# The w_out product by Strassen's scheme on half blocks, the last stage's operand split at its store, the forward transform in float32

## The chip, the cores and the metric

The kernel runs on one core of a Trainium2 chip. The metric is the device time of one execution in microseconds; beside it one execution is profiled. A core has a matrix engine (PE, with its weight loads shown apart as PEld), three engines for element-wise work (DVE, ACT, POOL), a queue engine (SP) that issues most transfers, and 16 DMA engines. Matmul results land in PSUM, which has eight banks of 512 float32 columns a partition; all else lies in SBUF. Each engine works through its own list of instructions in order and waits at semaphores.

## The reference

`x` is 8 x 3008 x 256, the two mixing matrices are 256 x 256, `w_in` is 256 x 2048 and `w_out` 2048 x 256, all float32.

```python
X = np.fft.rfft(x, axis=1)
Yr = Xr @ w_r - Xi @ w_i + b_r
Yi = Xr @ w_i + Xi @ w_r + b_i
Yr, Yi = shrink(Yr, 0.01), shrink(Yi, 0.01)     # sign(v) * max(|v| - 0.01, 0)
y = np.fft.irfft(Yr + 1j * Yi, n=3008, axis=1)
h = y.reshape(24064, 256) @ w_in
out = (np.maximum(h, 0.0) ** 2) @ w_out
```

## The kernel before

The transform over 3008 points is done as 64 x 47 points with matrices of cosines and sines. Per batch of 3008 tokens there are four stages. The **forward units** (`Fwd`) add and subtract mirrored inputs on POOL and multiply them with `am`; the result goes to the DRAM tensor `s1`. The **pairs** (`Pair`, twelve per batch) read it back, multiply with `bm`, mix with the weights (`mul`, `mix`), shrink, multiply with `cm` (`back`) and store to `s3`. The **last stage** (`Back`) reads `s3` as `du`, splits it, multiplies with `dx` and leaves `yt`, the transposed input of the feed-forward part. The **feed-forward part** takes tiles of 470 or 376 tokens, seven a batch, and for each tile the 2048 hidden columns in sixteen blocks of 128: `moe_h` multiplies with `win` into a `psh` bank, squares the positive part to `g`, and `moe_o` multiplies `g` with `wout` into two `pso` banks, one per half of the 256 output columns.

Products are made exact enough by splitting: an operand v becomes a rounded `fp32r` part (a cast on ACT) and the rest (a subtraction on DVE or POOL), and a product is three matmuls: high x high, low x high, high x low. So a block costs six matmuls with `win` and six with `wout`, each as wide as the tile.

Batch 0 runs its transform in plain float32 at the start, the front, together with the conversion of the 64-bit weights in 16 parts (`Double`): 12 of the parts are converted there, four beside the first tiles. From then on the tiles of batch b are the main line, and the pairs of batch b+1, the forward units of batch b+2 and the last stage of the next tile are jobs with due times in slots (one slot is one block) that are emitted between the blocks (`pair_tasks`, `fwd_tasks`, `back_tasks`). `moe_o` of a block follows `moe_h` by `LAG` = 2 blocks. A scheduler then sets each engine's order from this emission. The PSUM pools are two `psh` banks, two `pso` banks and four `psf` banks for all transform stages.

Of the kernel before, what the change touches and what calls it, by code (L numbers as in the profile page):

```python
# [29 lines left out]
TILES = (5, 4, 5, 4, 5, 4, 5)  # L30
NF = FF // 128
LAM = 0.01
LAG = 2
NP1 = N1 + 1
AHEAD = 12
FRONT = {"a32": 1, "b32": 1, "w320": 1, "w321": 1, "big": 5, "small": 5, "ka": 5, "xe": 4, "kv": 3}
MAIN = {"xt": 1, "xs": 1, "ksh": 1, "ksl": 1, "duh": 1, "dul": 1, "dy": 1, "xe": 1, "xl": 1, "kv": 1, "xh": 1, "kp": 1, "kq": 1, "mgh": 3, "mgl": 3}
# [3 lines left out]

@with_exitstack
def fnet_moe(ctx: ExitStack, tc, x, w_r, w_i, b_r, b_i, w_in, w_out, am, bm, cm, dm, dx, a32, c32, out):
# [4 lines left out]
    wk = ctx.enter_context(tc.tile_pool(name="wk", bufs=2))  # L48
    cv = ctx.enter_context(tc.tile_pool(name="cv", bufs=1))
    dram = ctx.enter_context(tc.tile_pool(name="dram", bufs=1, space=DRAM))  # L50
    ps_o = ctx.enter_context(tc.tile_pool(name="ps_o", bufs=1, space=PSUM))
    ps_h = ctx.enter_context(tc.tile_pool(name="ps_h", bufs=2, space=PSUM))
    ps_f = ctx.enter_context(tc.tile_pool(name="ps_f", bufs=4, space=PSUM))

    s1 = [dram.tile([G, NP1, 2, D], F32, name=f"s1_{b}") for b in range(B)]
    s3 = [dram.tile([M2, NP, D], F32, name=f"s3_{b}") for b in range(B)]

    am_sb = const.tile([M1, 2, 2, M1], F32R, name="am_sb")
    cm_sb = const.tile([128, G, 256], F32R, name="cm_sb")
    dm_sb = const.tile([M2, 2 * N2], F32, name="dm_sb")  # L60
# [4 lines left out]
    wout = [const.tile([128, NF, D], F32R, name=f"wout{j}") for j in range(2)]  # L65
# [3 lines left out]
    phase = {"pool": front.enter_context(tc.tile_pool(name="front", bufs=2)), "bufs": FRONT}  # L69

    def T(name, shape, dt, tag=None):
        tag = tag or name
        return phase["pool"].tile(shape, dt, name=name, tag=tag, bufs=phase["bufs"].get(tag, 2))

# [39 lines left out]
    def load_consts(g0, g1):  # L114
        pool.dma_start(cm_sb[:, g0:g1], cm[:, g0:g1])


    class Double:
        def __init__(self, hi, lo, src, ins):
            self.hi, self.lo, self.src, self.ins = hi, lo, src, ins  # L120

        def load(self):
            self.st = T("dst", [128, 512, 2], I32, tag="big")
            self.get = nc.sync.dma_start(self.ins(self.st), self.src)
            self.tile = lambda name, dt: T(name, [128, 512], dt, tag="small")

        def load_later(self):
            self.st = cv.tile([128, 512, 2], I32, name="dst", bufs=2)
            load_next(self.ins(self.st), self.src)
            self.tile = lambda name, dt: cv.tile([128, 512], dt, name=name)  # L130

        def bits(self, after):


            self.f = f = self.tile("df", I32)
            self.a = a = self.tile("da", F32)
# [11 lines left out]
        def join(self):  # L148
            self.w = w = self.tile("dw", F32)
# [6 lines left out]
        def split(self):  # L156
            w, hi = self.w, self.hi
            v = w.rearrange("p (f d) -> p f d", f=hi.shape[1]) if len(hi.shape) == 3 else w
            copy(act, hi, v)
            sub(dve, self.lo, v, hi)  # L160

    def moe_part(q):
        if q < 8:
            f, c = divmod(q, 2)
            fs = slice(f * 512, f * 512 + 512)
            return Double(
                win[0][:, c, fs], win[1][:, c, fs],
                w_in[c * 128:(c + 1) * 128, f * 1024:(f + 1) * 1024],
# [522 lines left out]
```

## Time and profile before

| | us |
|---|---|
| median of 3 runs | 2730.65 (2728.38 to 2730.72) |
| the profiled execution | 2727.27 |
| its span in the trace | 2725.5 |
| DVE busy | 1764.8 (65% of the span) |
| ACT busy | 1524.1 (56%) |
| POOL busy | 1058.6 (39%) |

A busy time is the sum of an engine's instructions; the span runs from the first to the last instruction of the program, and the execution takes 1.8 us more than it. A row of a group names the line, engine and operation, the tiles (output <- inputs), the shapes, the count, the busy time with the mean of one in ns, and then the idle time just before them with what ended it. A row of a timeline begins with the start and the length in us. A row of a stretch gives, for PE, PEld, DVE, ACT and POOL, busy us and instructions, then PE's granted clock, the share of the DMA engines and GB/s.

### The profile page before, as it was taken

The numbers are of one execution on the slowest core, as the hardware profiler recorded it, in microseconds if no ns is written. First come the engines' busy times: TensorE is split into PE (matmuls) and PEld (weight loads), VectorE is DVE, ScalarE is ACT, GpSimd is POOL, SyncE is SP. The second block draws the span as 40 slices with busy tenths as digits, with TensorE's granted clock in tenths as the row PEclk, the third lists the DMA queues.
The fourth block names the chain that finished last, engine by engine and source line by source line (L and its number), as shares of the span: only waits on it lengthen the run. The fifth ranks groups of instructions, "written<-read, shape, count | busy, mean of one in ns | idle before, by whom it ended". The sixth has DMA issues, their size and how long they took to land.

```text
span 2725.5 us, 41465 instructions
## 1 busy us (share of the span) xinstructions
PE 2682.9 (98%) x14902; PEld 2479.4 (91%) x14902; DVE 1764.8 (65%) x3050; ACT 1524.1 (56%) x3286; POOL 1058.6 (39%) x1071
## 2 busy tenths in 40 slices
PE   6899999999999999999999999999999999999999
PEld 5688999999999999899998999989999999999998
DVE  5956776667666676666666666666666666655554
ACT  3455565555565555555565555555555555555554
POOL 2144544444443443543534444344444343332200
PEclk8899999999999999999999999999999999999999
DMA  8443321222121221222211122122112111010000
GB/s 267 138 138 90 98 68 55 73 59 73 49 79 52 64 83 41 69 66 68 64 59 56 59 74 65 57 62 76 59 53 62 34 60 47 30 33 28 24 14 13
DMA packets 120356, 181.13 MB, mean 66 GB/s; under 512 B 12679, under 2 KB 90871, under 8 KB 119767
## 3 DMA queue, kind: packets, MB, share of 16 engines
q1 hardware_dynamic: 119271, 174.53, 21.1%
q0 software_dynamic: 880, 3.96, 0.5%
q8 instruction: 117, 1.92, 0.3%
q14 instruction: 88, 0.72, 0.1%
HBM read 103.07 MB, written 75.37 MB: 65 GB/s over the span
## 4 chain that ended last, share of the span: by engine, by line
PE 92%; DVE 3%; DMA 2%; issue 1%; POOL 1%; ACT 1%; SPq 0%; ACTq 0%; POOLq 0%; DVEq 0%
PE psh L458 38%; PE pso L480 38%; PE psf L263 7%; PE psf L240 3%; PE psf L297 2%; PE psf L215 2%; PE psf L439 1%; PE psf L434 1%; PE psf L438 1%; DMA xt<-x_in 1%; POOL xs L190 0%; DMA x<-x_in 0%; DVE df L143 0%; DVE dw L150 0%; DMA du<-s 0%
## 5 line engine op out<-in xcount | busy, mean ns | idle before, releaser
L458 PE MATMUL psh<-yt,win 128*128 128x470 f32 (+1 forms) x5376 | 1227.0, 362 | 1.7 <-DVE mg L466 1.1
L458 PEld LDWEIGHTS psh<-yt,win 128*128 128x128 f32 x5376 | 946.6, 189 | 70.3 <-DVE mg L466 3.4
L480 PE MATMUL pso<-mgh,wout 128*128 128x470 f32 (+1 forms) x3584 | 932.4, 359 | 0.0
L81 DVE TENSOR_TENSOR mgl<-mg,mgh 128x470 fp32r<-128x470 f32 (+1 forms) x896 | 650.3, 726 | 394.8 <-ACT mgh L77 367.5
L466 DVE SCALAR_TENSOR_TENSOR mg<-psh,mr 128x470 f32<-128x470 f32 (+1 forms) x896 | 539.8, 603 | 433.9 <-ACT mr L465 427.5
L77 ACT CAST mgh<-mg 128x470 fp32r<-128x470 f32 (+1 forms) x896 | 495.7, 553 | 473.8 <-DVE mg L466 469.8
L465 ACT ACTIVATE mr<-psh 128x470 f32<-128x470 f32 (+1 forms) x896 | 474.4, 530 | 419.4 <-PE psh L458 411.1
L480 PEld LDWEIGHTS pso<-mgh,wout 128*128 128x128 f32 x3584 | 653.8, 188 | 51.1 <-ACT mgh L77 0.2
L480 PE MATMUL pso<-mgl,wout 128*128 128x470 f32 (+1 forms) x1792 | 581.0, 359 | 1.0 <-DVE mgl L81 1.0
L480 PEld LDWEIGHTS pso<-mgl,wout 128*128 128x128 f32 x1792 | 328.5, 188 | 26.4 <-DVE mgl L81 1.7
L81 POOL TENSOR_TENSOR duh<-du,duh 32x512 fp32r<-32x512 f32 (+1 forms) x141 | 168.9, 1198 | 431.8 <-issue 255.1
L276 POOL TENSOR_TENSOR ke<-ke,bias 128x512 f32<-128x512 f32 x84 | 109.1, 1298 | 365.3 <-ACT ke L77 364.7
L81 POOL TENSOR_TENSOR dul<-du,duh 64x256 fp32r<-64x256 f32 x251 | 221.6, 883 | 31.6 <-PE psf L439 14.6
L263 PE MATMUL psf<-wx,kxh 128*128 128x256 f32 x1008 | 226.5, 282 | 0.0
L81 POOL TENSOR_TENSOR yt<-dy,yt 128x376 fp32r<-128x376 f32 (+1 forms) x141 | 134.9, 956 | 234.7 <-ACT yt L77 218.2
L190 POOL TENSOR_TENSOR xs<-xt 120x512 f32<-120x512 f32 (+1 forms) x98 | 131.4, 1340 | 176.9 <-DVE xl L81 74.2
L263 PEld LDWEIGHTS psf<-wx,kxh 128*128 128x128 f32 x1008 | 173.7, 188 | 6.8 <-ACT kxh L77 0.3
L253 POOL TENSOR_TENSOR kp<-kxh 128x256 f32<-128x256 f32 x84 | 65.9, 784 | 287.2 <-ACT kxh L77 259.2
L285 DVE TENSOR_TENSOR kv<-psf,ke 64x256 f32<-64x256 f32 x336 | 141.7, 422 | 30.5 <-PE psf L263 23.3
L263 PE MATMUL psf<-wx,kxl 128*128 128x256 f32 x504 | 141.6, 281 | 0.0
L443 DVE TENSOR_TENSOR dy<-psf,dy 128x188 f32<-128x188 f32 (+1 forms) x282 | 86.5, 325 | 27.6 <-ACT dy L77 22.5
L240 PE MATMUL psf<-kb,ka 128*128 128x128 f32 x672 | 104.0, 275 | 0.0
(85 smaller groups left out, 2398.9 us busy)
## 6 DMA issues: line engine op xcount, KB each, us to landing
s<-ku SPq DMA_DIRECT2D x192, 128.0 KB, 1.8
s<-xe SPq DMA_DIRECT2D x48, 480.0 KB, 3.3
du<-s SPq DMA_DIRECT2D x112, 192.0 KB, 3.0
ka<-s SPq DMA_DIRECT2D x84, 256.0 KB, 2.8
xt<-x_in SPq DMA_DIRECT2D x42, 480.0 KB, 5.3
out<-mo SPq DMA_DIRECT2D x64, 235.0 KB, 2.0
kb<-bm_in SPq DMA_DIRECT2D x84, 128.0 KB, 2.7
out<-mo SPq DMA_DIRECT2D x48, 188.0 KB, 2.0
```

The source lines that it names most:

```text
L77: return act.copy(out=out, in_=in_)
L81: return eng.tensor_tensor(out=out, in0=a, in1=b, op=ALU.subtract)
L190: return eng.tensor_tensor(out=out[:, :n], in0=self.xt[:, :n, 0], in1=self.xt[:, :n, 1], op=(ALU.add, ALU.subtract)[t])
L240: nc.tensor.matmul(pv[:, :, c, g, :], self.a[:, g, c * 128:(c + 1) * 128], bg, start=True, stop=True)
L263: self.last = nc.tensor.matmul(ps, l, wx[j][:, k, c, :], start=n == 0, stop=n == 5)
L276: pool.tensor_tensor(out=self.e, in0=self.e, in1=bias, op=ALU.add)
L285: dve.tensor_add(out=v[64 * r:64 * r + 64, g], in0=ps[gs], in1=self.e[gs, r])
L443: dve.tensor_add(out=y[:, c, :n * W], in0=ps[:, 0, :n * W], in1=y[:, c, :n * W])
L458: nc.tensor.matmul(ps[:, :k], win[w][:, c, fs], y[:, c, :k], start=n == 0, stop=n == 5)
L465: act.activation(r, ps[:, :k], AF.Relu)
L466: dve.scalar_tensor_tensor(out=g, in0=ps[:, :k], scalar=0.0, in1=r, op0=ALU.max, op1=ALU.mult)
L480: nc.tensor.matmul(acc[t][d][:, :k], wout[w][:, f, dsl], g, start=f == 0 and j == 0, stop=f == NF - 1 and j == 2,)
```

## The change

**The w_out product.** The sixteen blocks are taken as eight steps of two (`Step`), the tile's tokens as two halves of h = 252 or 250 (six tiles a batch, `HALF`), and the output as two halves of 128 columns. The 2 x 2 blocks of g (two hidden blocks by two token halves, side by side in `mc`) and of `wout` are multiplied by a scheme of seven products in place of eight: four with sums of g (`ms`: T1, T3, T2, T4, made by three POOL subtractions and additions; split into `mt`), three with plain parts (`mb`). The sums of `wout` (S1 to S4) are made once, in the front (`wout_sums`). The products are summed over the steps in four `pso` banks, and at a tile's end `drain` copies them out and forms the four output blocks by six POOL additions. So the psf banks go from four to two.

```diff
-    def moe_h(t, f):
...
-    def moe_o(t, f):
...
+    class Step:
+        def block(self, j):
...
+            if j == 0:
+                r = T("mr", [128, 2 * HM], F32)[:, :w]
+                act.activation(r, ps, AF.Relu)
+                dve.scalar_tensor_tensor(out=c, in0=ps, scalar=0.0, in1=r, op0=ALU.max, op1=ALU.mult)
+                return
+            act.activation(c, ps, AF.Relu)
+            act.activation(c, c, AF.Square)
...
+            halves(self.raw[0][:, B11], self.raw[1][:, B11], c[:, 0], dve)
+            halves(self.raw[0][:, B21:], self.raw[1][:, B21:], c[:, 2:4], dve)
+            self.s = s = T("ms", [128, 4 * HM], F32)[:, :4 * h].rearrange("p (j h) -> p j h", j=4)
+            pool.tensor_tensor(out=s[:, T1:T3 + 1], in0=c[:, 1::2], in1=c[:, 0:2], op=ALU.subtract)
+            pool.tensor_tensor(out=s[:, T2], in0=c[:, 0], in1=s[:, T3], op=ALU.add)
+            sub(pool, s[:, T4], c[:, 2], s[:, T2])
+        def split(self):
+            halves(self.sum[0], self.sum[1], self.s, dve)
+        def out(self, j):
...
+            products = (
+                ((A12, self.raw, B21, o[0], 0), (S4, self.raw, B22, o[0], 1), (A11, self.raw, B11, o[1], 0)),
+                ((S2, self.sum, T2, o[1], 1), (S1, self.sum, T1, o[2], 0), (S3, self.sum, T3, o[2], 1),
+                 (A22, self.sum, T4, o[3], 0)),
+            )[j]
+            for a, g, b, ps, i in products:
+                for k, (w, v) in enumerate(((0, 0), (1, 0), (0, 1))):
...
+                        mm = nc.tensor.matmul(
                            ps[:, i], wout[w][:, n, a], g[v][:, b], start=first and i == 0,
                            stop=n == NF // 2 - 1 and k == 2 and (i == 1 or a == A22),
                        )
+        def drain(self, j):
...
+            copy(act, e[:, 4:6], o[1])
+            copy(act, e[:, 6:8], o[2])
+            copy(dve, e[:, 2], o[3][:, 0])
...
+            add(u2, u2, p1)
+            add(c22, p5, p7)
+            add(e[:, 6:8], e[:, 6:8], u2.unsqueeze(1).broadcast_to([128, 2, h]))
+            add(e[:, 0:2], e[:, 0:2], e[:, 4::2])
+            add(c22, c22, u2)
+            add(e[:, 2], e[:, 2], p7)
```

`halves(hi, lo, v, eng)` is the cast on ACT and the subtraction on `eng`. The tile `ms` has one buffer, `mc`, `mb` and `mt` have two. `copy(dve, e[:, 0:2], o[0])` empties the first bank half a step earlier.

**The other edits.** `store_back` stores the result of `back` to `s3` already split (ACT cast, DVE subtraction from PSUM, two stores), so `Back.split` with its POOL subtractions goes and `Back.load` reads three pieces; the last stage always works on 188 columns and copies a piece that belongs to the next tile later (`put(1)`). `Fwd.run` multiplies in plain float32 (`am32`) without a split. In `Pair`, the bias is added by DVE from PSUM, the sum for the third product is formed from PSUM (ACT copy, DVE addition) in place of three POOL additions, the split after the shrink goes to POOL, and `cm` is loaded per pair by a transfer that POOL issues (`load_back`) and no longer kept. All 16 weight parts are converted in the front; the four sums of each pair of `wout` parts are four DVE operations of 128 x 256, followed by splits of 256, 512 and 1024 columns a partition. The due times and buffer counts are set anew:

```diff
-                first, step = 1.0, 7.5
+                first, step = 1.0, 6.1
-                    first, step = 31.0, 5.2
+                    first, step = 20.5, 4.6
-    jobs += fwd_tasks(b + 2, 0, 10.0 if b else 30.0, 6.8 if b else 5.0)
+    jobs += fwd_tasks(b + 2, 75.0, 1.4)
-                    jobs += back_tasks(t, tt * NF + 2.5)
+                    jobs += back_tasks(t, NF * j + 0.5)
-        k = n * 9 // 5
+        k = n * 13 // 10
```

**Where instructions now stand.** On PE, in the last batch of the kernel before, the products of a block (`pso`, with the casts `mgh` and the rests `mgl`) and the win product of a later block (`psh`) take turns, six and six:

```order
L480 MATMUL pso_29552<-mgh,wout_100 128x470
L480 MATMUL pso_29552<-mgh,wout_101 128x470
L480 MATMUL pso_29553<-mgh,wout_100 128x470
L480 MATMUL pso_29553<-mgh,wout_101 128x470
L480 MATMUL pso_29552<-mgl,wout_100 128x470
L480 MATMUL pso_29553<-mgl,wout_100 128x470
L458 MATMUL psh<-yt_29219,win_98 128x470
L458 MATMUL psh<-yt_29219,win_99 128x470
L458 MATMUL psh<-yt_29220,win_98 128x470
L458 MATMUL psh<-yt_29219,win_98 128x470
L458 MATMUL psh<-yt_29219,win_99 128x470
L458 MATMUL psh<-yt_29220,win_98 128x470
```

On PE in the last batch of the changed kernel, the products of one step's sums (`mt_32361` is the cast, `mt_32362` the rest) are parted by a whole win product:

```order
L515 MATMUL pso_32155<-mt_32361,wout_84 128x250
L515 MATMUL pso_32156<-mt_32361,wout_83 128x250
L515 MATMUL pso_32156<-mt_32361,wout_84 128x250
L473 MATMUL psh<-yt_32016,win_81 128x500
L473 MATMUL psh<-yt_32016,win_82 128x500
L473 MATMUL psh<-yt_32017,win_81 128x500
L473 MATMUL psh<-yt_32016,win_81 128x500
L473 MATMUL psh<-yt_32016,win_82 128x500
L473 MATMUL psh<-yt_32017,win_81 128x500
L515 MATMUL pso_32154<-mt_32362,wout_83 128x250
L515 MATMUL pso_32155<-mt_32362,wout_83 128x250
L515 MATMUL pso_32155<-mt_32361,wout_83 128x250
```

Counted over the whole order of before, the products of a block start after the win products of two later blocks in 855 of 896 cases, as the text of the program has it. In the changed kernel the plain parts `mb` of a step come two steps' win products after that step's start, but the sums' casts `mt` mostly 3.5 and their rests 4.0, where the text has 3.0.

On ACT before, in the last batch, the relu (`mr`) and the cast (`mgh`) alternate:

```order
L77 CAST mgh<-mg 128x376
L465 ACTIVATE mr<-psh 128x376
L77 CAST mgh<-mg 128x376
L465 ACTIVATE mr<-psh 128x376
L77 CAST mgh<-mg 128x376
L465 ACTIVATE mr<-psh 128x376
```

On ACT in the changed kernel, in the last batch, a step is six instructions, and the cast of the sums (`mt_32251`, of the step two before the one whose plain part is `mb_32359`) stands between the relus of the two blocks:

```order
L480 ACTIVATE mr<-psh 128x500
L89 CAST mb_32304<-mc 128x500
L89 CAST mt_32251<-ms 128x1000
L483 ACTIVATE mc<-psh 128x500
L89 CAST mb_32359<-mc 128x250
L484 ACTIVATE mc<-mc 128x500
L480 ACTIVATE mr<-psh 128x500
L89 CAST mb_32359<-mc 128x500
```

On POOL before, in a batch with pairs and forward units, all is work of the transform: `duh`, `dul` and `yt` of the last stage, `kp`, `kq`, `kxl` and `ke` of a pair, `xs` of a forward unit:

```order
L190 TENSOR_TENSOR xs<-xt 120x512
L81 TENSOR_TENSOR duh<-du,duh 32x256
L81 TENSOR_TENSOR dul<-du,duh 64x256
L81 TENSOR_TENSOR yt_21153<-dy,yt_21152 128x2x188
L276 TENSOR_TENSOR ke<-ke,bias 128x512
L81 TENSOR_TENSOR duh<-du,duh 32x512
```

On POOL in the changed kernel, at a tile's end in a batch with pairs, the three operations on `ms` of every step stand among the additions of `drain` (`me`), a load it issues (`kcm`) and the last stage's `yt`:

```order
L100 DMA kcm<-cm_in 128x512
L493 TENSOR_TENSOR ms<-mc 128x500
L494 TENSOR_TENSOR ms<-mc,ms 128x250
L93 TENSOR_TENSOR ms<-mc,ms 128x250
L539 TENSOR_TENSOR me<-me 128x250 x2
L539 TENSOR_TENSOR me<-me 128x500
L539 TENSOR_TENSOR me<-me 128x250
L493 TENSOR_TENSOR ms<-mc 128x500
L539 TENSOR_TENSOR me<-me 128x500
L539 TENSOR_TENSOR me<-me 128x250
L494 TENSOR_TENSOR ms<-mc,ms 128x250
L93 TENSOR_TENSOR ms<-mc,ms 128x250
```

The additions part the first operation on `ms` from the other two, which come before the cast on ACT.

More of the change, by code (lines that the diff above doesn't have):

```diff
@@ L561, in fnet_moe @@
     with tc.issue_after(ring[-1].folds[1].ins):
-        pool.dma_start(am_sb, am)
         pool.dma_start(dx_sb, dx)
-    chain.append(units[-1].get)
-    load_next(dm_sb, dm)
-    for p in parts[AHEAD:AHEAD + 2]:
-        p.load_later()
+    chain[nc.sync], chain[pool] = units[-1].get, ring[-1].folds[1]
+    front.close()
+    phase.update(
+        pool=ctx.enter_context(tc.tile_pool(name="main", bufs=2)), bufs={**MAIN, "psf": 2, "psh": 2},
+        psum=ctx.enter_context(tc.tile_pool(name="main_ps", bufs=1, space=PSUM)),
+    )
```

455 lines of the change are left out of this document (233 added, 222 removed).

## Prediction

> **What bounds the kernel now.** I read the page's busy line first, then the sums over a stretch in the middle, then the chain that ended last, then the groups.
>
> ```profile
> PE 2682.9 (98%) x14902; PEld 2479.4 (91%) x14902; DVE 1764.8 (65%) x3050; ACT 1524.1 (56%) x3286; POOL 1058.6 (39%) x1071
> 1000.00:1400.00 400.00, 400.00 (x2268) 372.33 (x2267) 263.04 (x449) 231.93 (x496) 172.15 (x173) 1.00 0.21 63
> PE 92%; DVE 3%; DMA 2%; issue 1%; POOL 1%; ACT 1%; SPq 0%; ACTq 0%; POOLq 0%; DVEq 0%
> L458 PE MATMUL psh<-yt,win 128*128 128x470 f32 (+1 forms) x5376 | 1227.0, 362 | 1.7 <-DVE mg L466 1.1
> L480 PE MATMUL pso<-mgh,wout 128*128 128x470 f32 (+1 forms) x3584 | 932.4, 359 | 0.0
> ```
>
> In the stretch from 1000 to 1400 us PE is busy for all 400 us at full granted clock (1.00), with DVE at 66%, ACT at 58%, POOL at 43% and the DMA engines at 21%. The chain is 92% PE. So the middle costs what its matmuls cost, and the first question is their pace. Ends of matmuls are modelled, so I take runs of one kind and divide the time by their number.
>
> ```profile
> 2530.54 2.60 PE psh L458 x12
> 2533.14 2.56 PE pso L480 x12
> 2494.93 2.07 PE psh L458 x12
> 330.38 1.42 PE psf L263 x12
> 64.67 0.61 PE L347 MATMUL psf<-kbb,ka 128*128 128x128 f32 x4
> 65.11 0.60 PE L372 MATMUL psf<-kv,kk 128*128 128x256 f32 x2
> 65.55 1.89 PE L361 MATMUL psf<-w,kx 128*128 128x256 f32 x8
> 67.27 0.61 PE L347 MATMUL psf<-kbb,ka 128*128 128x128 f32 x4
> 1531.01 0.28 PE L438 MATMUL psf<-dx_sb,duh 128*128 128x188 f32 x1
> 1531.12 0.27 PE L439 MATMUL psf<-dx_sb,dul 128*128 128x188 f32 x1
> ```
>
> 470 columns take 215 ns, 376 take 172, 256 take 118: 0.457 to 0.462 ns a column, though every matmul loads new weights. 188 columns take 110 ns (1531.01 to 1531.12), more than their share, so a floor lies just there. Plain float32 is two instructions per product, 215 ns each at 256 columns (eight from 65.55 to 67.27) and 110 at 128 (four from 64.67 to 65.11).
>
> **The change, part by part.** *PE.* win keeps its columns (24064 x 96). wout has as many before, 2.310 million, 1057 us at 0.4575. After it has 48 tiles x 8 steps x 21 matmuls of 252 or 250 columns, 2.021 million, at the 256-wide row's 0.462 ns 934 us: **-123 us**. The width is not in the trace; bounds are 110 ns (the 188 row) and 118 ns, 887 to 951 us. The forward product goes from six matmuls of 256 columns a unit to four float32 instructions: 91 x (4 x 215 - 6 x 118) ns = **+14 us**. The last stage keeps its matmuls nearly (784 to 768). PE's work behind the front is then win 1057, wout 934, pairs 84 x 3.7 = 312 (24 matmuls of 256 columns at 118, eight instructions at 110), forward 78, last stage 768 x 0.11 = 85: 2466 us.
>
> *Front.*
>
> ```profile
> 60.00:90.00 30.00, 28.89 (x152) 25.46 (x151) 29.89 (x75) 15.93 (x45) 0.00 (x0) 1.00 0.76 233
> 117.22 4.90 PE L458 MATMUL psh<-yt,win 128*128 128x470 f32 x12 [0.41 <-ACT yt L77]
> L143 DVE SCALAR_TENSOR_TENSOR df<-da,df 128x512 int32<-128x512 int32 x16 | 11.5, 717 | 0.1
> L142 DVE TENSOR_SCALAR da<-da 128x512 f32<-128x512 f32 x16 | 7.2, 452 | 2.2 <-ACT da L139 2.1
> L81 DVE TENSOR_TENSOR wout<-dw,wout 128x512 fp32r<-128x512 f32 x8 | 6.5, 818 | 0.3 <-ACT wout L77 0.3
> L81 DVE TENSOR_TENSOR kv<-kv,kc 128x256 f32<-128x256 f32 x24 | 10.0, 416 | 0.1
> ```
>
> DVE is full there (29.89 of 30), and the first win product starts at 117 us. All 16 weight parts now stand ahead of it, where 12 did: four more at six operations of 0.45 to 0.72 us, 3.6 together, make 14. Each pair of wout parts gets four 128x256 sums (0.42) and splits of 256, 512 and 1024 columns (0.42, 0.69, about 1.2), 4.0 us; four pairs are 16, for the six wout splits of 0.82 that go. With the two more win splits, DVE gains 27. Before 60 us it idles, which takes some: **+22 us**, between 10 and 30. The same work leaves the main part, where PE covered it: no gain there.
>
> *End.*
>
> ```profile
> 2717.77 3.65 PE pso L480 x17
> out<-mo SPq DMA_DIRECT2D x64, 235.0 KB, 2.0
> ```
>
> PE ends at 2721.4, 4 us before the span. Now the last step's sums and six POOL additions (5.5 us, priced below) stand between with nothing beside them: **+8 us**, 5 to 12. So far -123 + 14 + 22 + 8 = -79: 2646 of span, 2648 with the 1.8 us around it, **if PE stays as full as now**.
>
> *What must stay hidden.* A step (two blocks) needs, per the rows below, 2.8 us of POOL, 1.05 of ACT and 1.2 of DVE in one ring. The tile ms has one buffer: POOL's first subtraction of the next step waits until DVE has read the last sums, DVE waits for ACT's cast, ACT for POOL.
>
> ```profile
> L276 POOL TENSOR_TENSOR ke<-ke,bias x84: 1278/1292/1517, 236.2 to 2375.3; 128x512 f32<-128x512 f32 x84
> L253 POOL TENSOR_TENSOR kp<-kxh x84: 725/741/1192, 226.4 to 2360.8; 128x256 f32<-128x256 f32 x84
> L77 ACT CAST mgh<-mg 128x470 fp32r<-128x470 f32 x512 | 300.9, 588 | 292.5 <-DVE mg L466 290.5 <-PE pso L480 1.1
> L77 ACT CAST mgh<-mg 128x376 fp32r<-128x376 f32 x384 | 194.8, 507 | 181.3 <-DVE mg L466 179.3 <-PE pso L480 0.9
> L81 DVE TENSOR_TENSOR ksl<-kv,ksh x84: 675/692/1781, 243.1 to 2385.5; 128x512 fp32r<-128x512 f32 x84
> L81 DVE TENSOR_TENSOR mgl<-mg,mgh x896: 528/649/1740, 130.2 to 2719.8; 128x470 fp32r<-128x470 f32 x102, 128x376 fp32r<-128x376 f32 x78
> ```
>
> (The first two and the last two are views of one tile: minimum, median and maximum in ns.) POOL: 1.28 for 504 columns and twice 0.74 for 252. ACT: 0.86 ns a column between the two casts, so 1.05 at 1008 (two casts of 504, 1.24, would bound it). DVE: 0.69 at 512 and 0.42 at 256, so 1.21 at 1008 (at most 1.38 as two). Sum 5.0, with five hand-overs of about 0.05 5.3. But DVE and POOL do not run side by side:
>
> ```profile
> 1525.44 0.73 POOL L253 TENSOR_TENSOR kp<-kxh 128x256 f32<-128x256 f32 x1
> 1526.14 1.18 POOL L253 TENSOR_TENSOR kq<-kxl 128x256 f32<-128x256 f32 x1
> 1527.40 0.93 POOL L254 TENSOR_TENSOR kp<-kp,kq 128x256 f32<-128x256 f32 x1
> 1525.68 1.05 DVE L81 TENSOR_TENSOR xl<-xs,xh 120x512 fp32r<-120x512 f32 x1
> 1526.65 1.08 DVE L81 TENSOR_TENSOR mgl<-mg,mgh 128x376 fp32r<-128x376 f32 x1
> ```
>
> Five operations worth 0.74 + 0.69 + 0.74 + 0.53 + 0.74 = 3.44 us alone (mgl at 376 columns by its minimum) fill 1525.44 to 1528.33, 2.89 us: they take turns, and each change of turn gives back 0.14. DVE operations on PSUM do not stretch. The changed step adds 2.31 us of such DVE work (252, 504 and 1008 columns) to POOL's 2.8. DVE's two shorter subtractions fall into POOL's part of the ring: up to 0.82 us more, 5.3 to 6.1; I take the middle, **5.7 us a step**. The Trainium skill, "SBUF — State Buffer", section "Who interferes with whom", says that a DVE instruction with two SBUF inputs and a GpSimd one take a shared port by an exclusive lock for the whole instruction. The turns agree with that, the 0.14 us does not; held whole, it gives the fourth case below.
>
> At a tile's end POOL adds 4 x 0.74 + 2 x 1.28 = 5.5 us. While ACT and DVE work on ms (1.05 + 1.21), POOL has what DVE's turn leaves, some 1.2 us a step, so about 3 us of it lengthen the ring, 0.4 a step. Against this PE: 12 x 504 x 0.4575 + 21 x 252 x 0.462 = 5.21 us a step.
>
> Of 384 steps, by the tables of tasks, the pairs' tasks stand beside 246 (27 of batch 0, 36.5 of each of the next six), the forward units' beside 63 (nine, seven times), neither beside 75.
>
> - *No side work*: PE 5.43 with the last stage, ring 6.1: 0.67 x 75 = **+50 us**.
> - *Pairs*: 5.21 + 3.7/3.05 + 0.22 = 6.65. The ring 6.1, and POOL's further 1.2 us a step (kxl, ksl, yt, issuing a load) fit its free time or collide: 6.1 to 6.6. I take **0**, but this is thin.
> - *Forward units*: PE 6.67; POOL gets 13 x 2 x 0.74 = 19 us in nine steps, 2.1 a step, 0.9 over its room: ring 7.0. The order leaves the sums' products up to a step of slack, so **+10 us** of 22.
>
> Queued behind a waiting POOL subtraction are ksl, kxl, yt and the folds, and PE waits for each.
>
> ```profile
> L77 ACT COPY ke<-psf 128x512 f32<-128x512 f32 x84 | 49.2, 586 | 8.7 <-PE psf L263 7.5
> L115 POOL DMA_DIRECT2D cm_sb<-cm_in x3 | 1.7, 577 | 0.0
> ```
>
> Two psf banks in place of four cost nothing if jobs stay 0.9 slot (2.9 us) apart, since emptying a bank takes 0.6 to 1.4; if each pair stalls once, 84 x 0.6 = 50 us. The 84 loads issued by POOL (0.58 each) are in the 1.2 above. The doubled stores to s3 go to DMA engines that are 21% busy: nothing.
>
> Sum: 2648 + 50 + 10 = **2708 us**, beside 2727.3 of the profiled execution; the median of three, 2730.65, lies 3.4 above that.
>
> **The rivals.** *Everything is absorbed:* the ring runs at 5.3 and PE paces all stages, 2648. For it: no stretch of before shows PE waiting. Against it: the order puts the sums' products later than the program's text does, up to four steps' win products behind, where before they stood at their place.
>
> *The ring paces the pairs too* (slower): DVE carries 2.31 + 0.69 us a step and for each pair eleven operations of 0.42 to 0.69 us, 5.5 together, so 4.8 a step there, and each of its turns waits for POOL's; a late DVE subtraction delays POOL, which delays ACT. It decides from a ring of 6.75: (2733 - 2708) / 246 = 0.10 above 6.65. At 6.95 it costs 74 us, and some 8 more in the forward units: 2790. For it: turns stretch ksl from 0.69 to 1.78 us and mgl to 1.74 at worst, with POOL at 43%.
>
> ```profile
> L81 POOL TENSOR_TENSOR yt<-dy,yt 128x376 fp32r<-128x376 f32 (+1 forms) x141 | 134.9, 956 | 234.7 <-ACT yt L77 218.2
> L287 DVE TENSOR_SCALAR kc<-kv 128x512 f32<-128x512 f32 x84 | 41.5, 494 | 0.1
> ```
>
> *The turns are held whole* (the page's rule as a mechanism of this kernel): per step 2.31 + 2.76 + 0.69 of tile sums + 0.32 of yt (128 x 0.956 / 384) = 6.08, x 384 = 2335; pairs 84 x 3.2 = 270 (kxl 0.74, ksl 1.29, kv 0.69, kc 0.49); folds 135. 2740 behind a front of 139 and an end of 9: 2888. With 0.14 back at six turns a step it is under PE's 2466. The rows speak against it.
>
> *Two banks are too few:* 2708 + 50 = 2758.
>
> *The shorter products gain nothing*, because each weight load (188 ns in the groups) would pace them: the 256-wide row at 118 excludes it.
>
> **How the numbers follow.** Forecast 45% (its own range 2660 to 2730), absorbed 12%, ring in the pairs 28%, two banks 8%, turns held whole 6%, no gain 1%. Range: from the absorbed case, 2650, to a ring of some 7.1, 2830. A measurement of this kernel tells about 0.2% from no change (2725 to 2736). Faster: the absorbed case and nine tenths of the forecast, 0.52. The same: the edges, 0.09. Slower: 0.39.
>
> **What would show it.** wout groups at 8064 matmuls paced near 115 ns; the first win product near 139 us; windows in the pairs with PE over 97% busy and in the last batch near 89%, with PE's weight loads waiting for DVE mt; POOL near 75% busy with its 256-wide operations well above 0.74. It would be wrong if PE's share in the pairs fell below 94% (ring) or if PE waited there for ACT or DVE to empty psf (banks).

## The result, and the profile after

| | before | after |
|---|---|---|
| median | 2729.52 us (2728.08 to 2730.72) | 2941.26 us (2939.76 to 2944.61) |
| ratio | | 1.078 (95%: 1.076 to 1.080) |
| span of the profiled execution | 2725.5 | 2940.7 |

The kernel became 212 us slower. The forecast was 2708, the range ended at 2830. One execution is left out of all that follows, the second of experiment e5: it took 5440 us, twice as long as the first. The first fence is from the page of the changed kernel: the busy line, the engines of the chain that ended last, and three groups.

```profile
PE 2685.1 (91%) x16856; PEld 2406.9 (82%) x16856; DVE 2081.2 (71%) x3035; ACT 1789.2 (61%) x3562; POOL 2012.1 (68%) x2082
...
POOL 34%; PE 30%; DVE 15%; issue 8%; ACT 7%; DMA 1%; SPq 0%; POOLq 0%; DVEq 0%; ACTq 0%
...
L493 POOL TENSOR_TENSOR ms<-mc 128x500 f32<-128x500 f32 (+1 forms) x384 | 502.0, 1307 | 559.8 <-DVE mt L93 557.1
...
L481 DVE SCALAR_TENSOR_TENSOR mc<-psh,mr 128x500 f32<-128x500 f32 (+1 forms) x384 | 260.5, 678 | 387.5 <-POOL ms L93 368.6
...
L539 POOL TENSOR_TENSOR me<-me 128x250 f32<-128x250 f32 (+3 forms) x288 | 288.1, 1018 | 30.0 <-ACT me L89 23.3
```

The chain was 92% PE. Now POOL has 34% of it, and PE 30%, although POOL is busy for only 68% of the span: POOL stands idle for 557 us before L493, until DVE has read the last sums, and DVE for 369 us before L481, until POOL has read the buffer of `mc` that is to be overwritten. Engines that wait for each other hold the kernel with none of them full. The sums over stretches and the list of waits say what that does to PE:

```profile
1000.00:1400.00 400.00, 376.62 (x2432) 342.22 (x2432) 292.08 (x435) 252.37 (x504) 285.54 (x300) 0.97 0.30 89
160.00:2930.00 2770.00, 2584.35 (x16453) 2327.78 (x16452) 1971.28 (x2803) 1727.61 (x3404) 1952.64 (x2028) 0.97 0.27 79
```

```profile
POOL ms L493 <- DVE mt L93: 557.1, 255, 4.8
ACT mt L89 <- POOL ms L93: 474.0, 292, 5.9
DVE mc L481 <- POOL ms L93: 368.6, 258, 6.8
...
PE psh L473 <- DVE mc L481: 91.8, 81, 4.0
```

(A wait is given by total us, number of times and the longest.) The stretch from 1000 to 1400 us had PE busy for 400.00 of 400 at a clock of 1.00; now it is 376.62 at 0.97. From 160 to 2930 us PE is idle for 2770 - 2584 = 186 us. The last row, about half of that, is the end of the chain: `psh` has two banks, the win product needs one emptied by DVE (L481), DVE waits for POOL. The prediction's own sign of being wrong is there too. It named a share of PE under 94% beside the pairs: from 1000 us on it is 94.2%, and in the three stretches of 400 us behind that 92.4 to 92.7%.

**Where in the tile.** From the starts of POOL's first subtraction (L493) in the trace I took the time of every step, and the mean by its place in the tile (batches are counted from 0). The first two places are those beside which POOL forms the output of the tile before.

| mean step, us, by place | 1 | 2 | 3 | 4 | 5 | 6 | 7 | 8 | batch mean |
|---|---|---|---|---|---|---|---|---|---|
| after, batch 4 (pairs beside it) | 8.60 | 10.59 | 6.80 | 6.72 | 6.42 | 7.67 | 6.24 | 6.52 | 7.45 |
| after, batch 7 (nothing beside it) | 7.46 | 7.18 | 5.56 | 5.58 | 5.42 | 5.84 | 6.64 | 5.58 | 6.17 |

Beside the pairs, steps 3 to 8 take 6.7 on average, PE's own pace by the prediction (6.65). The loss stands in the first two. This is POOL's timeline over such a tile end (start, length, and in brackets the idle time before):

```profile
1279.03 1.40 POOL L493 TENSOR_TENSOR ms<-mc 128x504 f32<-128x504 f32 x1 [2.39 <-DVE mt L93]
1280.51 1.06 POOL L494 TENSOR_TENSOR ms<-mc,ms 128x252 f32<-128x252 f32 x1
1281.54 0.99 POOL L93 TENSOR_TENSOR yt<-dy,yt 128x376 fp32r<-128x376 f32 x1
1282.50 0.72 POOL L93 TENSOR_TENSOR ms<-mc,ms 128x252 f32<-128x252 f32 x1
1283.36 0.74 POOL L539 TENSOR_TENSOR me<-me 128x252 f32<-128x252 f32 x1
1285.32 0.80 POOL L539 TENSOR_TENSOR me<-me 128x252 f32<-128x252 f32 x1 [1.22 <-ACT me L89]
1286.08 1.27 POOL L493 TENSOR_TENSOR ms<-mc 128x504 f32<-128x504 f32 x1
1287.32 2.14 POOL L539 TENSOR_TENSOR me<-me 128x504 f32<-128x504 f32 x2
1289.41 0.91 POOL L494 TENSOR_TENSOR ms<-mc,ms 128x252 f32<-128x252 f32 x1
1290.29 1.18 POOL L93 TENSOR_TENSOR kxl<-kp,kxh 128x256 fp32r<-128x256 f32 x1
1291.42 2.37 POOL L539 TENSOR_TENSOR me<-me 128x504 f32<-128x504 f32 x2
1293.75 0.72 POOL L93 TENSOR_TENSOR ms<-mc,ms 128x252 f32<-128x252 f32 x1
1294.42 1.28 POOL L93 TENSOR_TENSOR ksl<-kv,ksh 128x512 fp32r<-128x512 f32 x1
1295.66 1.18 POOL L93 TENSOR_TENSOR yt<-dy,yt 128x8 fp32r<-128x8 f32 x1
1296.86 1.38 POOL L493 TENSOR_TENSOR ms<-mc 128x504 f32<-128x504 f32 x1
```

A step's three operations on `ms` are L493, L494 and L93. At 1279 they end 4.2 us after their start. At 1286 four tile-end additions (L539) and a pair's `kxl` stand in between, and they end 8.4 us after it; the steps that begin at 1279.03 and 1286.08 take 7.05 and 10.78 us. Only after the third may ACT cast, DVE subtract and L481 overwrite `mc`. These are the rows of PE, then of DVE, at that place:

```profile
1281.01 1.54 PE L473 MATMUL psh<-yt,win 128*128 128x504 f32 x6
...
1291.13 0.65 PE L515 MATMUL pso<-mb,wout 128*128 128x252 f32 x4
1293.32 0.77 PE L332 MATMUL psf<-ksh,kcm 128*128 128x256 f32 x4 [1.53 <-DVE dy L445]
1295.24 2.89 PE L473 MATMUL psh<-yt,win 128*128 128x504 f32 x6 [1.16 <-DVE mc L481]
...
1294.50 0.68 DVE L481 SCALAR_TENSOR_TENSOR mc<-psh,mr 128x504 f32<-128x504 f32 x1 [0.98 <-POOL ms L93]
```

POOL's third operation ends at 1294.47, DVE's L481 starts at 1294.50, and PE's win product follows. Its six matmuls take 2.89 us where six took 1.54 at 1281: the clock has fallen. (The first wait, 1.53 us before L332, is put down to DVE's `dy`, which empties a `psf` bank; it is not the ring's own.) The same place in stretches of 2 us, and in two rows cut where the clock changes (the third number from the end is the granted clock):

```profile
1290.00:1292.00 2.00, 1.78 (x16) 1.58 (x14) 2.00 (x2) 0.00 (x0) 2.00 (x3) 1.00 0.04 14
1292.00:1294.00 2.00, 0.68 (x4) 0.56 (x4) 0.62 (x3) 1.25 (x4) 2.00 (x3) 1.00 0.01 2
1294.00:1296.00 2.00, 0.84 (x3) 0.67 (x3) 1.12 (x2) 1.50 (x3) 2.00 (x3) 0.55 0.68 256
1296.00:1298.00 2.00, 2.00 (x7) 1.55 (x6) 1.11 (x2) 0.84 (x3) 1.99 (x2) 0.50 0.00 0
1298.00:1300.00 2.00, 2.00 (x10) 1.97 (x9) 0.68 (x1) 1.43 (x4) 0.24 (x1) 0.50 0.00 0
1300.00:1302.00 2.00, 2.00 (x10) 1.64 (x9) 0.76 (x2) 0.31 (x2) 1.76 (x3) 0.75 0.43 91
1302.00:1304.00 2.00, 2.00 (x20) 2.00 (x19) 1.29 (x2) 1.68 (x3) 0.29 (x1) 1.00 0.94 287
...
1290.80:1294.21 3.41, 1.75 (x13) 1.34 (x11) 1.82 (x4) 1.25 (x4) 3.41 (x4) 1.00 0.06 22
1294.21:1295.24 1.03, 0.00 (x0) 0.00 (x1) 0.68 (x1) 0.74 (x1) 1.03 (x2) 0.50 0.99 376
```

So a wait can cost twice: the idle time, and PE at half speed behind it, here for nearly 7 us. Not every wait does. In the trace's clock records the clock fell to 0.50 at 31 places between 165 and 2905 us, at 23 of them for 3.4 us, 137 us in all, while PE waited over 170 times.

### The profile page after: what moved, and what is told of

It is laid out like the page before. It is cut to its first block, busy times and chain, and to the rows that moved or that the text cites. A ratio compares the mean times of both kernels' runs of the same rounds, so it can differ in the third digit from the quotient of the medians.

```text
span 2940.7 us, 47049 instructions
## 1 busy us (share of the span) xinstructions
PE 2685.1 (91%) x16856; PEld 2406.9 (82%) x16856; DVE 2081.2 (71%) x3035; ACT 1789.2 (61%) x3562; POOL 2012.1 (68%) x2082
## 4 chain that ended last, share of the span: by engine, by line
POOL 34%; PE 30%; DVE 15%; issue 8%; ACT 7%; DMA 1%; SPq 0%; POOLq 0%; DVEq 0%; ACTq 0%
PE psh L473 14%; PE pso L515 10%; POOL ms L493 9%; POOL me L539 7%; DVE mt L93 6%; POOL ms L494 6%; POOL ms L93 6%; ACT mt L89 4%; PE psf L300 3%; POOL xs L232 3%; DVE kv L321 2%; DVE mb L93 2%; POOL ksl L93 2%; DVE mc L481 1%; POOL yt L93 1%
## 5 line engine op out<-in xcount | busy, mean ns | idle before, releaser
L473 PE MATMUL psh<-yt,win 128*128 128x500 f32 (+1 forms) x4608 | 1239.9, 404 | 93.6 <-DVE mc L481 91.8
L493 POOL TENSOR_TENSOR ms<-mc 128x500 f32<-128x500 f32 (+1 forms) x384 | 502.0, 1307 | 559.8 <-DVE mt L93 557.1
L93 DVE TENSOR_TENSOR mb<-mc,mb 128x500 fp32r<-128x500 f32 (+3 forms) x768 | 697.7, 918 | 136.2 <-ACT mb L89 132.9
L515 PEld LDWEIGHTS pso<-mt,wout 128*128 128x128 f32 x4608 | 653.6, 193 | 64.4 <-ACT mt L89 10.5
L515 PE MATMUL pso<-mt,wout 128*128 128x250 f32 (+1 forms) x4608 | 686.2, 285 | 9.9 <-ACT mt L89 8.4
L89 ACT CAST mt<-ms 128x1000 fp32r<-128x1000 f32 (+1 forms) x384 | 395.9, 1031 | 475.2 <-POOL ms L93 474.0
L93 DVE TENSOR_TENSOR mt<-ms,mt 128x1000 fp32r<-128x1000 f32 (+1 forms) x384 | 494.8, 1289 | 109.7 <-ACT mt L89 106.8
L515 PE MATMUL pso<-mb,wout 128*128 128x250 f32 (+1 forms) x3456 | 537.4, 284 | 21.2 <-DVE mb L93 21.1
L481 DVE SCALAR_TENSOR_TENSOR mc<-psh,mr 128x500 f32<-128x500 f32 (+1 forms) x384 | 260.5, 678 | 387.5 <-POOL ms L93 368.6
L515 PEld LDWEIGHTS pso<-mb,wout 128*128 128x128 f32 x3456 | 466.2, 189 | 35.1 <-DVE mb L93 26.1
L93 POOL TENSOR_TENSOR ms<-mc,ms 128x250 f32<-128x250 f32 (+1 forms) x384 | 314.4, 819 | 21.3
L494 POOL TENSOR_TENSOR ms<-mc,ms 128x250 f32<-128x250 f32 (+1 forms) x384 | 307.8, 802 | 22.0
L539 POOL TENSOR_TENSOR me<-me 128x250 f32<-128x250 f32 (+3 forms) x288 | 288.1, 1018 | 30.0 <-ACT me L89 23.3
L93 POOL TENSOR_TENSOR yt<-dy,yt 128x376 fp32r<-128x376 f32 (+3 forms) x168 | 153.1, 917 | 51.2 <-ACT yt L89 46.6
```

What stands on the lines that cost most here:

```text
L89: return act.copy(out=out, in_=in_)
L93: return eng.tensor_tensor(out=out, in0=a, in1=b, op=ALU.subtract)
L473: nc.tensor.matmul(ps, win[k][:, c, fs], y[:, c, :w], start=n == 0, stop=n == 5)
L481: dve.scalar_tensor_tensor(out=c, in0=ps, scalar=0.0, in1=r, op0=ALU.max, op1=ALU.mult)
L493: pool.tensor_tensor(out=s[:, T1:T3 + 1], in0=c[:, 1::2], in1=c[:, 0:2], op=ALU.subtract)
L494: pool.tensor_tensor(out=s[:, T2], in0=c[:, 0], in1=s[:, T3], op=ALU.add)
```

## The experiments

Three theories stood at the start. **Ring**: POOL's additions and sums, DVE's and ACT's splits and the one buffer of `ms` pace the steps. **Port**: POOL and DVE are slowed by each other's turns, whatever the buffers. **Banks**: two `psf` banks make the transform products wait. Ratios are to the kernel before.

| run | us (median) | ratio (95%) |
|---|---|---|
| e1, `ms` with two buffers | 2816.61 | 1.0323 (1.0293 to 1.0353) |
| e2, no tile-end additions | 2714.93 | 0.9945 (0.9923 to 0.9968) |
| e3, eight products, two `psf` banks | 2827.54 | 1.0363 (1.0333 to 1.0393) |
| e4, sums on DVE | 2780.24 | 1.0190 (1.0160 to 1.0219) |
| e5, three tile-end additions on DVE | 2747.07 (one execution) | |
| e6, e1 and e5 together | 2751.37 | 1.0074 (1.0045 to 1.0103) |
| e7, sums on DVE, a split on POOL | 2845.24 | 1.0418 (1.0388 to 1.0448) |
| e8, eight products, four `psf` banks | 2732.76 | 1.0010 (0.9999 to 1.0021) |
| e10, e5 again | 2750.35 | 1.0080 (1.0064 to 1.0097) |
| e11, four tile-end additions on DVE | 2767.31 | 1.0141 (1.0126 to 1.0156) |
| e12, eight products, three `psf` banks | 2732.97 | 1.0016 (1.0007 to 1.0026) |
| e13, after, another order | 2945.22 | 1.0790 (1.0774 to 1.0806) |
| e14, after, a third order | 2943.89 | 1.0784 (1.0768 to 1.0800) |
| e15, e11 in another order | 2773.26 | 1.0159 (1.0144 to 1.0174) |
| e16, e10 in another order | 2805.76 | 1.0279 (1.0262 to 1.0296) |
| e17, e2 in another order | 2709.32 | 0.9925 (0.9910 to 0.9940) |
| e18, e3 in another order | 2826.27 | 1.0352 (1.0337 to 1.0367) |
| e19, e8 in another order | 2732.69 | 1.0011 (1.0002 to 1.0021) |

**e1: `ms` with two buffers** (`ka` and `kcm` give up one each for the room).

```diff
-    ... "mr": 1, "ms": 1, "me": 1,
+    ... "mr": 1, "ms": 2, "me": 1, "ka": 1, "kcm": 1,
```

> Changed kernel with two buffers for ms (room made by one buffer in place of two for ka and kcm, whose loads stay 2.4 and 1.8 slots behind the last read). No work is removed. Ring theory (POOL's three operations on ms, ACT's cast, DVE's subtraction and the wait for the one buffer set the step, and POOL's tile-end additions lengthen it): a step of the last batch falls from 5.72 us to PE's 5.4, the two steps at a tile's end (8.5 and 10 us now, others 6.6) lose part of their excess; 2740 to 2850 us. Port theory (POOL and DVE operations taking turns fill the time, whatever the buffers): the sum of turns is the same, 2900 to 2960.

2817, 125 under after: the ring, and not the turns by themselves, since no operation was taken away and both engines were busy for longer than in after (POOL 2080 us for 2012, DVE 2115 for 2081). 87 of the 212 us stay. My reading, not tried by itself: a second buffer lets one step's sums begin before the last are read, but the additions still stand in POOL's list.

**e2: the six additions at a tile's end left out.**

```diff
-            add(u2, u2, p1)
-            add(c22, p5, p7)
-            add(e[:, 6:8], e[:, 6:8], u2.unsqueeze(1).broadcast_to([128, 2, h]))
-            add(e[:, 0:2], e[:, 0:2], e[:, 4::2])
-            add(c22, c22, u2)
-            add(e[:, 2], e[:, 2], p7)
```

> Changed kernel without the six POOL additions of a tile's end: the output is made of single products. Ring theory: the two long steps at a tile's end (8.5 and 10 us) become ordinary (6.6), 48 x about 5 us = 200 to 250 less, 2690 to 2750 us. Prediction's own step (POOL's additions absorbed beside pairs): only the 75 steps without side work gain, 75 x 0.4 = 30 us, about 2910. Bank theory (PE waits for two psf banks): nothing changes, 2930 to 2945.

2715: **226 us less**, 4.7 us for each of the 48 tiles, with `ms` at one buffer and `psf` at two banks as they were. This run alone would fit the port theory too, since 5.5 us of POOL's work a tile are gone with their turns; e1 and the rows above speak for the ring. The busy line and the main stretch of this run:

```profile
PE 2602.3 (96%) x16856; PEld 2358.9 (87%) x16856; DVE 1996.1 (74%) x3035; ACT 1798.6 (66%) x3562; POOL 1730.4 (64%) x1794
```

```profile
160.00:2700.00 2540.00, 2496.82 (x16434) 2276.03 (x16432) 1883.56 (x2800) 1735.18 (x3402) 1671.59 (x1742) 1.00 0.29 86
```

The matmuls that kept PE busy for 2584 us behind the front take 2497 here, at a clock of 1.00, and PE idles for 2540 - 2497 = 43 us in place of 186. So the 226 us are, within a few us, 143 of waiting and 87 of PE being busy for longer over the same matmuls. The clock accounts for some 65 of these 87: the clock records of these stretches have 142 us at half speed in after and 11 here, and half of the difference is lost. The other 22 are not shown; the ends of matmuls are modelled, so short waits may hide in busy time. The mean step at places 1 and 2 of batch 4 is 6.91 and 6.60 (8.60 and 10.59 in after), the batch mean 6.67 (7.45), and that of batch 7 5.73 (6.17).

**e3, e8, e12: eight products, with two, four and three `psf` banks.** The scheme is undone, all else stays: each step multiplies the four plain blocks with `wout` (twelve matmuls of 504 or 500 columns) into two `pso` banks.

```diff
-            products = (
-                ((A12, self.raw, B21, o[0], 0), (S4, self.raw, B22, o[0], 1), (A11, self.raw, B11, o[1], 0)),
-                ((S2, self.sum, T2, o[1], 1), (S1, self.sum, T1, o[2], 0), (S3, self.sum, T3, o[2], 1),
-                 (A22, self.sum, T4, o[3], 0)),
-            )[j]
+            products = (((A11, 0, o[0]), (A12, 2, o[0])), ((S1, 0, o[1]), (A22, 2, o[1])))[j]
...
-        ... bufs={**MAIN, "psf": 2, "psh": 2},
+        ... bufs={**MAIN, "psf": 4, "psh": 2},
```

(`S1` holds a plain copy there; the last two lines are e8's, with 3 in e12.)

> Changed kernel with the w_out product by eight half-block products in place of seven (12 matmuls of 504 or 500 columns a step, two pso banks, all of g split as it comes, no ms, no mt, no additions at a tile's end); one of the four wout sums is replaced by a copy. All other edits stay. If Strassen's sums are what costs: PE paces again, 157 us of front + 2589 of PE work + about 1.3% + 6 = 2770 to 2800 us. If the other edits (two psf banks, float32 forward, split at the store, cm loads by POOL) hold PE up: over 2850.

> As e3 (eight products), with four psf banks as before the change. The run e3 lay 40 us above PE's own sum. Bank theory: those are waits for two psf banks and the half clock behind them, 2780 to 2805 us. Otherwise 2815 to 2835.

> The eight-product kernel of e3 (2827.5 with two psf banks, 2732.8 with four) with three. If two banks cost because a transform product must wait for the one before last to be emptied, a third bank takes away most of it: 2735 to 2755. If the cost rises evenly with each bank taken away: 2775 to 2785.

e3 fell between the two theories, at 2828, with POOL hardly loaded and no ring at all. e8 took 95 us off that by banks alone, more than expected, and e12 shows that the third bank is the one that counts. First come three of PE's waits in e3 that e8 does not have at all, then the main stretch of e3, then that of e8:

```profile
PE psf L279 <- DVE dy L445: 11.1, 8, 1.4
PE psf L235 <- ACT xe L89: 7.4, 6, 1.4
PE psf L300 <- DVE kul L93: 5.7, 6, 1.0
```

```profile
160.00:2800.00 2640.00, 2588.23 (x12913) 2190.05 (x12912) 1304.86 (x2313) 1495.52 (x3003) 495.51 (x593) 0.99 0.28 82
```

```profile
160.00:2720.00 2560.00, 2560.00 (x12976) 2186.74 (x12975) 1306.61 (x2323) 1490.59 (x3018) 509.19 (x594) 1.00 0.29 85
```

All three are products into a `psf` bank that DVE or ACT has still to empty (`dy`, `xe` and `kul` are formed from one). With four banks PE is busy for all of 2560 us; with two it idles for 52 of 2640, and its clock is lower (0.99 for 1.00).

**e4 and e7: the three operations on `ms` by DVE**; e7 also gives POOL the subtraction of the second plain split.

```diff
-            pool.tensor_tensor(out=s[:, T1:T3 + 1], in0=c[:, 1::2], in1=c[:, 0:2], op=ALU.subtract)
-            pool.tensor_tensor(out=s[:, T2], in0=c[:, 0], in1=s[:, T3], op=ALU.add)
-            sub(pool, s[:, T4], c[:, 2], s[:, T2])
+            dve.tensor_tensor(out=s[:, T1:T3 + 1], in0=c[:, 1::2], in1=c[:, 0:2], op=ALU.subtract)
+            dve.tensor_tensor(out=s[:, T2], in0=c[:, 0], in1=s[:, T3], op=ALU.add)
+            sub(dve, s[:, T4], c[:, 2], s[:, T2])
```

```diff
-            halves(self.raw[0][:, B21:], self.raw[1][:, B21:], c[:, 2:4], dve)
+            halves(self.raw[0][:, B21:], self.raw[1][:, B21:], c[:, 2:4], pool)
```

> Changed kernel with the three operations on ms done by DVE in place of POOL. Ring theory: the ring shrinks to 1.5 + 1.05 + 1.2 us and POOL's tile-end additions leave it; PE or DVE (about 6.5 us a step beside pairs) paces, 2720 to 2830 us. Port theory: the turns' sum falls by POOL's 2.8 us and rises by DVE's 1.5 a step, 384 x 1.3 = 500 us less, so PE paces as well: 2700 to 2760. Bank theory: no gain, 2920 or more.

> As e4 (operations on ms done by DVE), and in exchange the rest of the last two plain parts (500 columns) is subtracted by POOL and not by DVE: DVE loses 0.68 to 1.06 us a step, POOL gains 1.28 on a path with two steps of slack. In e4 DVE was busy 89%. If DVE paced e4: 2690 to 2740 us. If the ring through ACT paced it: 2765 to 2790.

e4 is 161 us faster than after, though DVE goes to 89% busy. The tile-end additions on POOL no longer stand in the ring, and the three operations take some 1.5 us on DVE in place of 2.8; the run does not tell the two apart. e7 missed both of its forecasts. It is slower than e4 by 65. In its trace POOL waited 471 us for ACT's cast before the rests of the plain parts, which PE needs earlier than the sums; that this is the cause was not tried.

**e5, e6, e10, e11: tile-end additions by DVE, straight from PSUM.** e5 (and e10, the same kernel) leaves two of six to POOL, e6 adds the two buffers of e1, e11 leaves one (the second cut has what e11 changes beyond e5).

```diff
-            copy(act, e[:, 6:8], o[2])
-            copy(dve, e[:, 2], o[3][:, 0])
...
-            add(c22, p5, p7)
-            add(e[:, 6:8], e[:, 6:8], u2.unsqueeze(1).broadcast_to([128, 2, h]))
+            dve.tensor_add(out=e[:, 6:8], in0=o[2], in1=u2.unsqueeze(1).broadcast_to([128, 2, h]))
+            dve.tensor_add(out=e[:, 2], in0=o[3][:, 0], in1=p7)
+            dve.tensor_add(out=c22, in0=o[2][:, 0], in1=p7)
...
-            add(c22, c22, u2)
-            add(e[:, 2], e[:, 2], p7)
```

```diff
-            copy(act, e[:, 4:6], o[1])
+            copy(act, e[:, 4], o[1][:, 0])
...
-            add(u2, u2, p1)
+            dve.tensor_add(out=u2, in0=o[1][:, 1], in1=p1)
```

> Changed kernel with three of a tile end's additions taken from POOL by DVE, straight from PSUM (the ACT copy of the third bank and one DVE copy go; POOL keeps one addition of 250 and one of 500 columns, 2.0 us in place of 5.5). Ring theory: of the 4.7 us that a tile's end costs by the run without additions, 3.5/5.5 go, 48 x 3.0 = 145 less: 2780 to 2830 us. If the cost lay in the waiting for PSUM to be emptied and not in POOL's additions: 2920 to 2960.

> The two remedies together: two buffers for ms, and POOL's tile-end additions cut to 2.0 us as in e5. Ring theory: 2817 of the two buffers less 40 to 100: 2715 to 2775 us. Port theory: as e5 alone.

> The kernel of the run e5_drain_dve once more, unchanged, for a ratio: at a tile's end DVE adds straight from PSUM and POOL is left with two additions (0.74 + 1.28, 2.0 us) in place of six (5.5 us). Ring at the tile's end: 2747 again, within 5 us, a ratio of 1.004 to 1.009.

> As e10, and one more tile-end addition (u2, 252 columns, 0.74 us of POOL) goes to DVE, which takes it straight from PSUM; ACT's copy before it is half as wide. POOL keeps one addition of 504 columns per tile, and the two DVE additions that need u2 no longer wait for POOL. Leaving all six POOL additions out gave 4.7 us a tile, moving 3.5 us of them 4.0. If the POOL additions in the ring are the cost, another 0.3 to 0.6 us a tile goes: 15 to 30 us, 2718 to 2733. If what is left at the tile's end is the emptying of the four banks (PE waiting for pso), nothing goes: 2742 to 2752.

Taking 3.5 of POOL's 5.5 us out of the tile end gave 191 us back (e10, 2750), more than I expected of e5; its steps at places 1 and 2 of batch 4 are 8.03 and 6.16. A second buffer on top gave nothing (e6). e11 missed both of its forecasts: 15 to 30 us faster or no change were on record, and it came out 17 slower. Its steps at places 1 and 2 are 7.07 and 7.54, and the others moved both ways. Every edit lets the scheduler write all rows anew, so I asked how much of these differences is the order.

**e13 to e19: the order alone.** The same kernels with the due times of the last stage's tasks 0.4 of a slot later; e14 has the forward units' 0.3 later instead.

```diff
-                    jobs += back_tasks(t, NF * j + 0.5)
+                    jobs += back_tasks(t, NF * j + 0.9)
```

```diff
-                jobs += fwd_tasks(b + 2, 75.0, 1.4) + [(95.0, pairs[b + 2][0].load)]
+                jobs += fwd_tasks(b + 2, 75.3, 1.4) + [(95.0, pairs[b + 2][0].load)]
```

> The changed kernel with the same work, and only the due times of the last stage's tasks 0.4 of a slot later (0.9 in place of 0.5): the scheduler then writes PE's and POOL's rows in another order. It shows how far the order alone moves the time, since every experiment so far changed the order too. If the differences between the experiments are their edits: within 25 us of 2941. If they are the luck of the order: 50 us or more away, and then the 226 us of the left-out additions are not shown to be theirs.

> The changed kernel with the same work, and only the due times of the forward units 0.3 of a slot later (75.3 in place of 75.0), a smaller change of the order than in e13. Edits: within 15 us of 2941. Luck of the order: 30 us or more away.

> The kernel of e11 (u2 on DVE, 2767.3) with the last stage's due times of e13. If e11 lost its 17 us against e10 by its order: 2735 to 2760. If by the edit itself: 2760 to 2780, and 10 us or more above e16.

> The kernel of e10 (three tile-end additions by DVE from PSUM, 2750.4) with the last stage's due times of e13. Edits: 2735 to 2765. Luck of the order: outside of that.

> The kernel of e2 (the six POOL additions at each tile's end left out, so the output is made of single products) with the last stage's due times of e13, for another order. If the 226 us are the additions' cost: 2700 to 2770, still 170 us or more under 2945. If much of them was luck of e2's order: above 2800.

> The kernel of e3 (eight products, two psf banks, 2827.5) with the due times of e13. If two banks cost 95 us: 2800 to 2850. If e3 had a bad order: under 2780.

> The kernel of e8 (eight products, four psf banks, 2732.8) with the due times of e13. With PE waiting for nearly nothing after the front, the order should matter little: 2728 to 2740.

The changed kernel stays where it was (2945 and 2944 for 2941). The additions are worth 226 us in one order and 2945.22 - 2709.32 = 236 in the other; the two banks 94.8 and 93.6. These two hold. But e10's kernel moves by 55 us (2806), out of the range that its edits should have kept it in, and e15 is 33 us *faster* than e16 where e11 was 17 slower than e10. So differences of some tens of us among the kernels with mended tile ends (e5, e6, e10, e11) are not shown to be their edits. e1, e4 and e7 were run in one order each, and their differences can hold as much of it.

## Why the prediction was wrong

**What was right.** *The shorter product.* The gain was put at 123 us of PE, from 934 us for the 8064 matmuls with `wout`. In after and in e2 their starts are 116 to 117 ns apart in the median: 8064 x 0.116 = 935 us. e2 against e3, which share the two `psf` banks and hold PE up about equally (some 94 us over their matmuls at median pace, worked out from the starts in both traces), is 113 faster. *The ring's own length.* 5.7 us were taken for a step with no side work. In the last batch of the changed kernel L493 starts at 2701.84, 2707.75 and 2713.47, and the median of that batch is 5.72. As the 5.7 was the middle of a range from 5.3 to 6.1, its closeness is partly luck:

```profile
2701.84 1.37 POOL L493 TENSOR_TENSOR ms<-mc 128x504 f32<-128x504 f32 x1 [2.38 <-DVE mt L93]
2703.30 0.73 POOL L494 TENSOR_TENSOR ms<-mc,ms 128x252 f32<-128x252 f32 x1
2704.10 1.26 POOL L93 TENSOR_TENSOR ms<-mc,ms 128x252 f32<-128x252 f32 x1
2707.75 1.39 POOL L493 TENSOR_TENSOR ms<-mc 128x504 f32<-128x504 f32 x1 [2.39 <-DVE mt L93]
2713.47 1.38 POOL L493 TENSOR_TENSOR ms<-mc 128x504 f32<-128x504 f32 x1 [2.39 <-DVE mt L93]
```

The 2.39 us of idle time are ACT's cast and DVE's subtraction, and the 1.26 in place of 0.73 stands beside a DVE subtraction (2704.09 to 2704.77), a turn as the prediction has it. *The additions with no side work.* 0.4 us a step were taken, for a ring of 6.1; e2 against after in that batch is 6.17 - 5.73 = 0.44.

**What was wrong: the pairs.** The step that failed is "Pairs ... The ring 6.1, and POOL's further 1.2 us a step ... fit its free time or collide: 6.1 to 6.6. I take **0**", which it called thin. The comparison was of means: a ring of 6.6 at most under PE's 6.65. The additions do not come as a mean. Six of them, and the pair's own POOL work, fall into two of eight steps and stand between the operations of the ring in POOL's list, so those steps take 8.6 and 10.6 us. The other six run at PE's pace and give nothing back; by my reading, since PE cannot run ahead of two `psh` banks. The batch means of after less those of e2, times 48 steps, sum to 224 us over the eight batches: 21 in the last, as priced, and 203 in the other seven, where the sum had 0 for the pairs, 10 for the forward units and some 11 (27 x 0.4) for the steps there without side work.

**The second wrong step: half speed.** I priced a wait at its length. Some 65 of the 226 us are PE at half speed behind waits. In the stretches of before that the prediction read there were no such waits to learn it from.

**The rivals.** *The ring paces the pairs too* had the right chain and the right sign, but not what lengthens it. Its price, 74 us over 246 steps or 0.30 a step, was half of the 0.60 that came (203 over the 336 steps of the seven batches), and it was laid to DVE's and POOL's turns in every step, not to two steps of each tile. *Turns held whole* gave 2888 and was nearer by its number, but its mechanism does not fit: e1 took no work off either engine, both were busy for longer, and it gained 125 us. (e4 does not decide it. On DVE the three operations are shorter, and the busy times of the two engines fell together from 4093 to 3412 us.) *Two banks*: "cost nothing" was wrong for a kernel with eight products (94 to 95 us, e8 and e19). In the seven-product kernel all eight banks are taken, so it could not be tried there, and what two banks cost in it stays open. e2 gives a bound: from its first win product to its last matmul it takes 2552 us, against 2458 for its matmuls at their median pace in the trace, so all that holds PE up there comes to 94 us, whatever its cause. (The 43 us of idle time are less than that, since busy time hides short waits.)

**The front**, a third term that was too small, was to end at 139 us, between 127 and 147. It ended at 157.66, 40 us later than before where 22 were taken. Rows of before, then of after (the first win product of before, 117.22, stands above):

```profile
105.92 0.70 PE L372 MATMUL psf<-kv,kk 128*128 128x256 f32 x2 [1.32 <-DVE kv L81]
111.64 3.70 PE L423 MATMUL psf<-dm_sb,du 96*128 96x94 f32 x16 [5.02 <-ACT win L77]
```

```profile
139.07 0.70 PE L404 MATMUL psf<-kv,kk 128*128 128x256 f32 x2 [2.82 <-DVE kv L93]
146.84 0.49 PE L439 MATMUL psf<-dx_sb,du 128*128 128x188 f32 x1 [7.07 <-DMA du<-s]
157.66 4.44 PE L473 MATMUL psh<-yt,win 128*128 128x504 f32 x12
```

DVE's added work moved the last unit by 33 us, not 22, and the way from there to the first win product grew from 11.3 to 18.6. That was read from the rows, not tried.

**The whole, from the runs.** Going from e8 over e3 and e2 to after: +95 for two banks in place of four, -113 for the seven products, +226 for forming the output on POOL. The sum is 208, 2941 less e8's 2733, as it must be, since neighbouring steps share a run: it is one path, not a check, and the 95 were measured with eight products. e2, which leaves the additions out, is only 18 us faster than e8. The other edits together, front included, leave the time where it was (e8, 1.001); what they gave back for the later front was not taken apart. No version that does all of the work was faster than the kernel before.

## What to carry to other kernels

When work goes to an engine with time to spare, don't compare its mean load with the bottleneck's: lay out the engine's list at the place where the work bunches, count the chain of hand-overs with that work inside it, and compare this step with the time that the bottleneck's buffers can bridge. Allow for a wait of the matrix engine to cost more than its length. And before reading a difference of one or two per cent between kernels whose order a scheduler writes, move the order alone and see how far the time goes.

## What the runs showed of the hardware

The granted clock fell to half without one long idle stretch. It fell at 1294.2, before the second of the two waits shown had more than begun: in the 3.41 us before, PE was busy for 1.75 and idle for 1.66, of which one wait of 1.53. It was back between 1300 and 1302, nearly 7 us after it fell. A longer wait elsewhere, 1118.80 to 1121.80 with PE busy for 0.01 of 3.00 us, left the clock at 1.00; what sets the two apart was not tried. The Trainium skill, "TensorE: Matmul & The Clock Gate", section "Part 1: The HAM clock gate (the "warmup" mystery)", has the clock at half after one idle window of about 3.4 us and back after one busy window; the two states agree with the rows here (0.50 and 1.00), but in this trace 1.66 us of idle time within the 3.41 us before the fall were enough. A POOL subtraction of 8 columns took 1.18 us (1295.66) while DVE held a subtraction of 1.21. And with eight products a third `psf` bank was worth as much as a third and a fourth: 2733 us for both, 2828 with two.
